# Attention and a rational feed-forward layer on one core: the numerator's constant is added on VectorE in the first part's units

## The chip, the cores and the metric

The kernel runs on one core of one Trainium2 chip. The core has a matrix engine (TensorE, "PE" in the profile; its weight loads are "PEld"), VectorE ("DVE"), ScalarE ("ACT"), GpSimd ("POOL") and SyncE ("SP", which only issues transfers). Each has its own list of instructions, which it works off in order; semaphores join the lists. SBUF is the on-chip memory, PSUM the memory into which TensorE writes, and the DRAM scratch tiles lie off the core.

The metric is device time in microseconds (us), lower is better. Before the change the median of 3 runs is 1245.48 us (1244.66 to 1249.6).

## The reference

Two layers, one behind the other. First block-causal attention over 8 batches of 8 heads, 576 positions, 64 numbers a head, with blocks of 64; then a feed-forward layer whose activation is a quotient of polynomials:

```
scores = q @ k.T / 8, masked where block(i) < block(j)
attn   = softmax(scores) @ v                 -> x, 4608 tokens x 512

h = x @ w_in                                 (512 -> 2048)
P = a[0] + a[1]*h + a[2]*h^2 + a[3]*h^3
Q = 1 + |b[0]|*|h| + |b[1]|*h^2
g = P / (Q + 1e-6)
out = g @ w_out                              (2048 -> 512)
```

## The kernel before

**Precision.** TensorE's fast format for fp32 keeps fewer bits than fp32. So nearly every operand x is held as a rounded part x_hi in that format and a remainder x_lo, and a product is three matmuls: hi by hi, hi by lo, lo by hi. For x, w_in and w_out these pairs are made once; for g they are made in each unit, as the tiles gh and gl.

**Attention.** 32 pairs of heads follow each other (p = 0 to 31). For each pair there are five row tiles and two halves, that is ten steps: scores on TensorE, the negative row maximum on VectorE (L542 to L548), the exponential on ScalarE (L560), the sums' reciprocal (L567 to L569) and the scaling on GpSimd (L572), a transposition on TensorE (L598), the split of the transposed tile on ScalarE (L611) and VectorE (L612), and the product with v on TensorE (L664), whose result is split again (L666, L667, L671) and stored to DRAM scratch xscr. The first EV = 5 pairs do without the split (L609, L621, L625). `bank` gives a PSUM tile to transpositions and to the preparation of the next pair: for p < LEND it goes in turn to the attention pool and to the two output banks o0 and o1, later to the attention pool alone.

**Feed-forward.** The 16 blocks of 128 hidden columns fall into two parts. The first part (ph = 0) is blocks 0 to 9, over chunks of 256 tokens, two blocks to a unit: 14 chunks of 5 units, 70 units, with a [128, 512] tile each. Its partial sums go to DRAM scratch pscr. The second part (ph = 1) has 74 units over chunks of 512 tokens, and runs behind attention. The units' steps are a generator, `Ffn.steps`, two half steps to a unit. A unit goes through `first` (24 matmuls of w_in, L229, and the start of P and Q), one unit later `recip`, two units later `split`, three units later `second` (the matmuls with w_out, L299).

The chain of one unit of the first part, in the names of the code, with h in PSUM and ut, vt, st tiles in SBUF:

```
first:  ACT  L236 ut = |h|         ACT L238 st = a3*h + a2     ACT L239 vt = b1*ut + b0
        POOL L243 ut = vt*ut       DVE L244 st = st*h          DVE L245 st = (st + a1)*h
recip:  ACT  L251 vt = Ln(ut + QC) ACT L258 vt = Exp(-vt)      (vt = 1/Q)
        ACT  L259 st = st + a0     DVE L260 gh = st*vt         (rounded)
        DVE  L261 ut = (ut + QC)*gh    POOL L263 ut = st - ut  (P - Q*gh)
split:  POOL L275 gl = ut*vt
second: PE   L299 o += gh.w_hi, gh.w_lo, gl.w_hi
```

In the second part the branch of `recip` is another one, and the change leaves it alone.

**What sets the order.** The loop over attention's steps emits half steps of `Ffn.steps` between them. Their number by a given step is a straight line, which ends at U1, where HOLD half steps are left out; what is held back is emitted after attention and works while the last pair's data is on its way:

```
E0, E1, U1 = there[0][0], there[-2][0], there[-2][1] * units_of(0, 0) * 2 - HOLD
```

The order of emission is not yet the order of execution. The kernel is built with `tile.TileContext(nc, schedule_with_timeline_sim=True)`: a planner with costs of its own for each instruction puts the lists of the engines in order and sets the semaphores. So an edit of one operation can move others, too. All transfers of attention and of the units are issued from SP's list (L214 loads a unit's x, L401 and L403 the next pair's q and k).

Of the kernel before, what the change touches and what calls it, by code (L numbers as in the profile page):

```python
# [8 lines left out]
F32 = mybir.dt.float32  # L9
# [3 lines left out]
AF = mybir.ActivationFunctionType  # L13
ALU = mybir.AluOpType
# [8 lines left out]
NCH = NT // CT  # L23
NF = DFF // 128
ALAG2 = 1
LEND = 4
RL = 3
C0 = 0
TP = 0
RW = 4  # L30
EV = 5
DP = 4
DN = (3, 0, 0, 0, 0)
KQB = 3
XB = 3
WR, WF = 1, 4
HOLD = 4
ALAG3 = 10
OFFS = (0,3,5)
TLAG = 6  # L40
# [27 lines left out]
QC = 1.0 + 1e-6  # L68
# [5 lines left out]
def attn_ffn_kernel(  # L74
# [11 lines left out]
    nc = tc.nc  # L86
# [27 lines left out]
    a0, a1 = coef[:, 0:1], coef[:, 1:2]  # L114
# [69 lines left out]
    class Ffn:  # L184
# [64 lines left out]
        def recip(self, ph, c, u):  # L249
            pool, ut, vt, st = self.m[ph, c, u]  # L250
            nc.scalar.activation(out=vt, in_=ut, func=AF.Ln, bias=qcb)  # L251
            tag = f"{ph}_{c}_{u}"
            gh, gl = (pool.tile([128, NBU[ph], CTS[ph]], F32R, name=f"g{x}{tag}", tag=f"g{x}",
                                bufs=GBUFS if pool is ffn else 2) for x in "hl")
            gf = gh.rearrange("p j t -> p (j t)")
            self.g[ph, c, u] = (gh, gl)
            if ph == 0:
                nc.scalar.activation(out=vt, in_=vt, func=AF.Exp, scale=-1.0)  # L258
                nc.scalar.activation(out=st, in_=st, func=AF.Identity, bias=a0)  # L259
                nc.vector.tensor_tensor(out=gf, in0=st, in1=vt, op=ALU.mult)  # L260
                nc.vector.scalar_tensor_tensor(out=ut, in0=ut, scalar=QC, in1=gf.bitcast(F32),  # L261
                                               op0=ALU.add, op1=ALU.mult)
                nc.gpsimd.tensor_tensor(out=ut, in0=st, in1=ut, op=ALU.subtract)  # L263
            else:
                r0 = ps_b.tile([128, 512], F32, name=f"r{tag}", tag="a", bufs=3)
                nc.scalar.activation(out=r0, in_=vt, func=AF.Exp, scale=-1.0)
                nc.vector.scalar_tensor_tensor(out=ut, in0=ut, scalar=QC, in1=r0, op0=ALU.add, op1=ALU.mult)
                nc.vector.scalar_tensor_tensor(out=r0, in0=ut, scalar=-2.0, in1=r0, op0=ALU.add, op1=ALU.mult)
                nc.vector.scalar_tensor_tensor(out=st, in0=st, scalar=a0, in1=r0, op0=ALU.subtract, op1=ALU.mult)
# [92 lines left out]
    with ExitStack() as actx:  # L362
# [27 lines left out]
        def load(p):  # L390
# [4 lines left out]
            tr = att.tile([128, 2, D], F32, name=f"tr{p}", tag="tr", bufs=1)  # L395
            if p >= EV:
                vr = att.tile([128, 2, 5, D], F32, name=f"vr{p}", tag="vr", bufs=1)
            for i, (raw, src) in enumerate(((qr, q), (kr, k))):
# [4 lines left out]
                eng.dma_start(out=tr[64 * i:64 * i + 64], in_=src[b, h0:h0 + 2, 512:S, :].rearrange("j p d -> p j d"))  # L403
            if p < EV:
                st_[p] = dict(qr=qr, kr=kr, tr=tr)
# [63 lines left out]
        def vprep(p):  # L469
            if p < EV:  # L470
                b, hp = divmod(p, NPAIR)
# [5 lines left out]
                return  # L477
            if p == EV:
                late()
# [13 lines left out]
        def bank(p, name):  # L493

            if p < LEND:
                nbank[0] += 1
# [92 lines left out]
        def transp(p, d):  # L589
            st_[p].pop(d)  # L590
            for gi, g in enumerate(groups(d)):
# [4 lines left out]
                for x, (i, h, kb) in enumerate(g):  # L596
                    src = pts[4] if i == 4 else pts[i][:, h]
                    nc.tensor.transpose(ps[:, 128 * x:128 * x + 128], src[:, 128 * kb:128 * kb + 128], ident)  # L598
                if p < EV:
                    if "pt" not in st_[p]:  # L600
# [6 lines left out]
                src = ps[:, :128 * n].rearrange(sh.get((g[0][0], n), "p (h k t) -> p h k t"), **kw)  # L607
                if p < EV:
                    nc.scalar.copy(out=spot(st_[p]["pt"], g), in_=src)  # L609
# [185 lines left out]
```

## Time and profile before

| | |
|---|---|
| median of 3 runs | 1245.48 us |
| the profiled execution's own time | 1246.05 us |
| its span, first to last instruction | 1244.3 us |
| PE busy / DVE / ACT / POOL | 1191.3 / 921.3 / 908.5 / 876.7 us |
| granted TensorE clock, mean | 0.994 |
| transferred | 145.67 MB, mean 117 GB/s |

The profile is of one execution. A group's row names its line, engine, operation, tiles (written <- read), shapes, count, then busy us and mean ns of one, then the idle time of the engine ahead of it and what ended that. A row of waits is "who <- for whom: us in total, times, longest". The chain of waits is followed back from the last instruction, at each step to what released it or to the instruction ahead of it on its engine. Matmuls are pipelined, so that their busy times overlap and a busy PE isn't PE at its peak.

### The profile page before, as it was taken

How to read it: one execution, taken by the hardware profiler on the slowest of the kernel's cores; microseconds unless marked ns; L12 is line 12 of the kernel's file. 1: busy time of each engine (PE TensorE's matmuls, PEld its weight loads, DVE VectorE, ACT ScalarE, POOL GpSimd, SP SyncE). 2: the span in 40 equal slices, each digit the busy share in tenths (PEclk: the TensorE clock that was granted, in tenths of full speed). 3: DMA queues.
4: the chain of work that ended last, by engine and by line, in shares of the span. 5: the costliest groups of instructions: out<-in, count | busy, mean ns of one | idle time of the engine just before them, and what ended most of it. 6: DMA issues, size and time to landing. Idle time of an engine off the chain costs nothing.

```text
span 1244.3 us, 21931 instructions
## 1 busy us (share of the span) xinstructions
PE 1191.3 (96%) x7124; PEld 1008.8 (81%) x7124; DVE 921.3 (74%) x2016; ACT 908.5 (73%) x2025; POOL 876.7 (70%) x1043
## 2 busy tenths in 40 slices
PE   6888999999999999999999999999999999999998
PEld 4666888888888878888888888878888888888886
DVE  6878888777888777877777777647666766677764
ACT  6877888877988878888888888756555655555554
POOL 4666778877888877787777877756665656665664
PEclk8999999999999999999999999999999999999999
DMA  8782344463544545443333342444014344443100
GB/s 233 208 232 71 94 138 113 121 179 89 143 114 132 132 125 143 108 136 100 100 103 92 105 110 68 113 154 189 1 64 131 120 136 136 136 136 102 43 1 34
DMA packets 199506, 145.67 MB, mean 117 GB/s; under 512 B 136288, under 2 KB 164960, under 8 KB 199392
## 3 DMA queue, kind: packets, MB, share of 16 engines
q1 hardware_dynamic: 196624, 143.15, 40.1%
q10 hardware_dynamic: 2704, 1.11, 0.3%
q8 instruction: 57, 0.93, 0.3%
q14 instruction: 57, 0.47, 0.1%
q0 software_dynamic: 64, 0.00, 0.0%
HBM read 92.28 MB, written 41.94 MB: 108 GB/s over the span
## 4 chain that ended last, share of the span: by engine, by line
PE 71%; ACT 8%; POOL 7%; DVE 5%; DMA 5%; issue 3%; SPq 1%; POOLq 0%; ACTq 0%; DVEq 0%
PE h L229 28%; PE o L299 26%; PE o L664 5%; PE t L598 4%; PE s L530 4%; ACT p L560 2%; PE o L625 2%; POOL gl L275 2%; DMA xt<-xh 1%; POOL u L263 1%; PE tp L438 1%; POOL p L572 1%; PE s L513 1%; DMA wri<-in_moe_w_in_dram 1%; DMA x<-xscr 1%
## 5 line engine op out<-in xcount | busy, mean ns | idle before, releaser
L229 PE MATMUL h<-x,wpi 128*128 128x256 f32 (+1 forms) x2568 | 453.6, 324 | 7.2 <-DMA x<-xscr 2.5
L229 PEld LDWEIGHTS h<-x,wpi 128*128 128x128 f32 x2568 | 380.7, 190 | 53.0 <-issue 6.0
L299 PE MATMUL o<-wpo,gh 128*128 128x512 f32 x1152 | 343.8, 395 | 0.0
L299 PEld LDWEIGHTS o<-wpo,gh 128*128 128x128 f32 x1152 | 212.8, 188 | 43.3 <-issue 0.7
L299 PE MATMUL o<-wpo,gl 128*128 128x512 f32 x576 | 210.3, 400 | 8.6 <-POOL gl L275 8.2
L572 POOL TENSOR_SCALAR p<-p,rc 128x128 f32<-128x128 f32 (+4 forms) x288 | 176.1, 623 | 48.4 <-DVE rc L569 32.9
L243 POOL TENSOR_TENSOR u<-v,u 128x512 f32<-128x512 f32 x144 | 187.5, 1302 | 13.2 <-ACT v L239 5.4
L560 ACT ACTIVATE p<-s,nm 128x288 f32<-128x288 f32 (+4 forms) x320 | 168.3, 534 | 25.2 <-DVE nm L548 19.9
L251 ACT ACTIVATE v<-u,qcb 128x512 f32<-128x512 f32 x144 | 105.1, 730 | 82.0 <-POOL u L243 81.7
L244 DVE TENSOR_TENSOR s<-s,h 128x512 f32<-128x512 f32 x144 | 98.5, 684 | 86.4 <-ACT s L241 65.2
L236 ACT ACTIVATE u<-h 128x512 f32<-128x512 f32 x144 | 86.4, 600 | 102.3 <-PE h L229 96.2
L548 DVE TENSOR_REDUCE nm<-s 128x1 f32<-128x128 f32 (+4 forms) x288 | 129.4, 474 | 7.4 <-PE s L513 4.7
L278 POOL TENSOR_TENSOR gl<-s,gh 128x512 fp32r<-128x512 f32 x74 | 95.8, 1294 | 55.0 <-ACT gh L277 54.9
L598 PE MATMUL t<-ident,p 128*128 128x128 f32 x800 | 122.5, 279 | 8.6 <-POOL p L572 4.1
L299 PEld LDWEIGHTS o<-wpo,gl 128*128 128x128 f32 x576 | 104.7, 189 | 31.1 <-POOL gl L275 12.4
L611 ACT CAST ptrh<-t 128x512 fp32r<-128x512 f32 (+1 forms) x189 | 98.4, 542 | 36.9 <-PE t L598 36.6
L612 DVE TENSOR_TENSOR ptrl<-t,ptrh 128x512 fp32r<-128x512 f32 (+1 forms) x189 | 115.5, 627 | 11.5 <-ACT ptrh L611 10.4
L242 POOL TENSOR_SCALAR v<-u,bab 128x512 f32<-128x512 f32 x74 | 57.2, 774 | 91.0 <-ACT u L236 90.9
L598 PEld LDWEIGHTS t<-ident,p 128*128 128x128 f32 x800 | 91.0, 141 | 27.8 <-POOL p L572 6.8
L263 POOL TENSOR_TENSOR u<-s,u 128x512 f32<-128x512 f32 x70 | 90.3, 1290 | 30.3 <-DVE u L261 16.2
L245 DVE SCALAR_TENSOR_TENSOR s<-s,coef,h 128x512 f32<-128x512 f32 x144 | 106.2, 738 | 2.4
L530 PE MATMUL s<-k,q 64*128 64x512 f32 (+3 forms) x768 | 86.4, 343 | 6.6 <-ACT p L560 2.9
(110 smaller groups left out, 2031.5 us busy)
## 6 DMA issues: line engine op xcount, KB each, us to landing
x<-xscr SPq DMA_DIRECT2D x44, 256.0 KB, 4.0
xscr<-xl SPq DMA_DIRECT2D x32, 288.0 KB, 2.4
out_dram<-os SPq DMA_DIRECT2D x34, 256.0 KB, 3.3
qr<-in_q_dram SPq DMA_DIRECT2D x64, 128.0 KB, 2.8
kr<-in_k_dram SPq DMA_DIRECT2D x62, 128.0 KB, 2.5
xt<-xh SPq DMA_DIRECT2D x54, 144.0 KB, 2.3
xscr<-xh SPq DMA_DIRECT2D x54, 144.0 KB, 2.5
pscr<-os SPq DMA_DIRECT2D x14, 512.0 KB, 2.7
```

The source lines that it names most:

```text
L229: nc.tensor.matmul(h[:, j, :], lhsT=w.win(f, dc, y), rhs=xs[dc][:, hl, :], start=(dc == 0 and i == 0), stop=(dc == 3 and i == 2))
L243: nc.gpsimd.tensor_tensor(out=ut, in0=vt, in1=ut, op=ALU.mult)
L245: nc.vector.scalar_tensor_tensor(out=st, in0=st, scalar=a1, in1=hf, op0=ALU.add if ph == 0 else ALU.subtract, op1=ALU.mult)
L251: nc.scalar.activation(out=vt, in_=ut, func=AF.Ln, bias=qcb)
L263: nc.gpsimd.tensor_tensor(out=ut, in0=st, in1=ut, op=ALU.subtract)
L299: nc.tensor.matmul(self.o[m], lhsT=g[:, j, ms], rhs=w.wout(f, y), start=(u == 0 and j == 0 and i == 0), stop=(u == nu - 1 and j == NBU[ph] ...
L530: mm = nc.tensor.matmul(s["s", t, h], lhsT=q[hs, x, 128 * t:128 * t + 128], rhs=k[hs, y, 0:128 * (t + 1)], start=(n == 0 and t == i), stop ...
L548: nc.vector.reduce_max(out=nm[:, j:j + 1], in_=s[d, j][:, :w] if i == 4 else s["s", i, j], axis=AX.X, negate=True)
L560: nc.scalar.activation(out=dst, in_=s.pop((d, j2))[:, :w] if i == 4 else s.pop(("s", i, j2)), func=AF.Exp, bias=nm[:, n:n + 1], scale=1.0, ...
L572: nc.gpsimd.tensor_scalar(out=x, in0=x, scalar1=rc[:, j2:j2 + 1], scalar2=1.0, op0=ALU.mult, op1=ALU.mult)
L598: nc.tensor.transpose(ps[:, 128 * x:128 * x + 128], src[:, 128 * kb:128 * kb + 128], ident)
L612: nc.vector.tensor_tensor(out=dl, in0=src, in1=dh.bitcast(F32), op=ALU.subtract)
```

## The change

In the first part's `recip`, st is no longer brought to P by an addition of its own. The two places that read P now read st and add a0 (a column of coef) themselves: the product that gives gh, and the subtraction that gives the remainder, which moves from GpSimd to VectorE. The ScalarE addition and the GpSimd subtraction are left out. `u % FUM < FUN` with both at 1 holds for every unit, so the old branch is never built. Two constants of the order are changed with it: LEND from 4 to 5 and HOLD from 4 to 3.

```diff
-LEND = 4
+LEND = 5
...
+FUM = 1
+FUN = 1
...
-HOLD = 4
+HOLD = 3
...
             if ph == 0:
                 nc.scalar.activation(out=vt, in_=vt, func=AF.Exp, scale=-1.0)
-                nc.scalar.activation(out=st, in_=st, func=AF.Identity, bias=a0)
-                nc.vector.tensor_tensor(out=gf, in0=st, in1=vt, op=ALU.mult)
-                nc.vector.scalar_tensor_tensor(out=ut, in0=ut, scalar=QC, in1=gf.bitcast(F32),
-                                               op0=ALU.add, op1=ALU.mult)
-                nc.gpsimd.tensor_tensor(out=ut, in0=st, in1=ut, op=ALU.subtract)
+                if u % FUM < FUN:
+                    nc.vector.scalar_tensor_tensor(out=gf, in0=st, scalar=a0, in1=vt, op0=ALU.add, op1=ALU.mult)
+                    nc.vector.scalar_tensor_tensor(out=ut, in0=ut, scalar=QC, in1=gf.bitcast(F32),
+                                                   op0=ALU.add, op1=ALU.mult)
+                    nc.vector.scalar_tensor_tensor(out=ut, in0=st, scalar=a0, in1=ut, op0=ALU.add, op1=ALU.subtract)
+                else:
+                    (the four lines above, as they were)
```

More of the change, by code (lines that the diff above doesn't have):

```diff
@@ L258, in recip @@
                 nc.scalar.activation(out=vt, in_=vt, func=AF.Exp, scale=-1.0)
-                nc.scalar.activation(out=st, in_=st, func=AF.Identity, bias=a0)
-                nc.vector.tensor_tensor(out=gf, in0=st, in1=vt, op=ALU.mult)
-                nc.vector.scalar_tensor_tensor(out=ut, in0=ut, scalar=QC, in1=gf.bitcast(F32),
-                                               op0=ALU.add, op1=ALU.mult)
-                nc.gpsimd.tensor_tensor(out=ut, in0=st, in1=ut, op=ALU.subtract)
+                if u % FUM < FUN:
[4 more added lines that the diff above has]
+                else:
+                    nc.scalar.activation(out=st, in_=st, func=AF.Identity, bias=a0)
+                    nc.vector.tensor_tensor(out=gf, in0=st, in1=vt, op=ALU.mult)
+                    nc.vector.scalar_tensor_tensor(out=ut, in0=ut, scalar=QC, in1=gf.bitcast(F32),
+                                                   op0=ALU.add, op1=ALU.mult)
+                    nc.gpsimd.tensor_tensor(out=ut, in0=st, in1=ut, op=ALU.subtract)
             else:
```

## The prediction

> **What bounds it now.** I read the page's totals and its chain first, then the busy time by stretch, then the groups of the lines that the change edits, then who waits for whom.
>
> ```profile
> span 1244.3 us, 21931 instructions
> PE 1191.3 (96%) x7124; PEld 1008.8 (81%) x7124; DVE 921.3 (74%) x2016; ACT 908.5 (73%) x2025; POOL 876.7 (70%) x1043
> PE 71%; ACT 8%; POOL 7%; DVE 5%; DMA 5%; issue 3%; SPq 1%; POOLq 0%; ACTq 0%; DVEq 0%
> ```
>
> The first two are the page's totals, the third the chain of waits by engine. The mean says "TensorE-bound", but it averages two stages. The 70 units that the change touches lie between 104 and 836 us, beside attention (rows below). The busy time by stretch (start and end, length, then busy us and instructions of PE, PEld, DVE, ACT and POOL, clock, DMA) separates the stages:
>
> ```profile
> 104.00:822.00 718.00, 694.01 (x4792) 605.24 (x4791) 566.06 (x1378) 592.66 (x1420) 561.24 (x700) 1.00 0.42 113
> ...
> 822.00:846.00 24.00, 21.42 (x104) 17.21 (x103) 10.22 (x15) 12.81 (x22) 13.44 (x12) 1.00 0.87 292
> 846.00:1244.00 398.00, 392.92 (x1734) 325.02 (x1732) 267.77 (x395) 223.46 (x365) 242.44 (x218) 1.00 0.27 90
> ```
>
> After 846 us TensorE works 392.92 of 398 us and every helper has room; nothing of the change runs there. From 104 to 822 us TensorE shows 694.0 of 718 us, and the three helpers stand close together: ScalarE 82.5%, VectorE 78.8%, GpSimd 78.2%. TensorE's busy time flatters it, since matmuls overlap. The chain of waits, asked for 104 to 846 us, gives its first lines their shares of 742 us:
>
> ```profile
> by line: PE h L229 20.1%; PE o L299 16.8%; PE o L664 8.5%; PE t L598 5.8%; PE s L530 5.6%; issue 3.2%; POOL gl L275 2.7%; DMA xt<-xh 2.4%; ACT p L560 2.3%; POOL u L263 2.2%; PE tp L438 2.0%; POOL p L572 1.6%; PE s L513 1.4%; POOL xl L671 1.
> ```
>
> The TensorE entries sum to about 60%, so some 40% of this stage is paced by other engines. L263, the GpSimd subtraction that the change takes away, is 2.2% of 742 us, 16.3 us, and L275, which runs behind it, another 20 us. So the stage is a balanced pipeline in which GpSimd's tail of each unit matters.
>
> **The operations.** These are the groups, with count, busy time, mean ns of one, and idle before:
>
> ```profile
> L244 DVE TENSOR_TENSOR s<-s,h 128x512 f32<-128x512 f32 x144 | 98.5, 684 | 86.4 <-ACT s L241 65.2 <-ACT s L238 20.7
> L245 DVE SCALAR_TENSOR_TENSOR s<-s,coef,h 128x512 f32<-128x512 f32 x144 | 106.2, 738 | 2.4
> L259 ACT ACTIVATE s<-s,coef 128x512 f32<-128x512 f32 x70 | 51.6, 738 | 9.9 <-DVE s L245 9.7
> L260 DVE TENSOR_TENSOR gh<-s,v 128x512 fp32r<-128x512 f32 x70 | 58.8, 840 | 17.1 <-ACT v L258 16.4
> L261 DVE SCALAR_TENSOR_TENSOR u<-u,gh 128x512 f32<-128x512 f32 x70 | 58.8, 840 | 2.3 <-DVE gh L260 0.9
> L263 POOL TENSOR_TENSOR u<-s,u 128x512 f32<-128x512 f32 x70 | 90.3, 1290 | 30.3 <-DVE u L261 16.2
> L275 POOL TENSOR_TENSOR gl<-u,v 128x512 fp32r<-128x512 f32 x70 | 91.0, 1300 | 2.3
> ```
>
> and the single-line views' smallest, median and largest duration:
>
> ```profile
> L244 DVE TENSOR_TENSOR s<-s,h x144: 662/686/691, 100.6 to 1229.4; 128x512 f32<-128x512 f32 x144
> L245 DVE SCALAR_TENSOR_TENSOR s<-s,coef,h x144: 661/746/750, 101.8 to 1230.1; 128x512 f32<-128x512 f32 x144
> L260 DVE TENSOR_TENSOR gh<-s,v x70: 666/693/2270, 106.6 to 833.4; 128x512 fp32r<-128x512 f32 x70
> L261 DVE SCALAR_TENSOR_TENSOR u<-u,gh x70: 665/693/2144, 107.4 to 834.2; 128x512 f32<-128x512 f32 x70
> ```
>
> Two things are to be seen. An operation whose added number comes from a column of coef (L245) has a median of 746 ns, one with a constant in the instruction (L261) 693. And L244, which reads one operand from PSUM, never strays beyond 691 ns, while L260 and L261, which read both from SBUF, average 840 - 693 = 147 ns over their median and reach 2270: now and then they are held up while running.
>
> *Removed on ScalarE:* 70 x 738 ns = 51.6 us (L259). It lies beside VectorE's and TensorE's work, and the exponential L258, not L259, is what L260 is seen waiting for. I take 0; the bounds are 0 and the 9.7 us in which ScalarE stood waiting for L245 ahead of L259.
>
> *Removed on GpSimd, added on VectorE:* 70 x 1290 ns = 90.3 us go. The new operation adds a column of coef and has both tensors in SBUF, a pairing that this trace does not hold; its bounds are L245's median of 746 ns and 746 + 147 = 893 ns, and I take 893 because its sources are L261's. That is 62.5 us. L260 becomes of that form too: 693 to 746, 53 ns x 70 = 3.7 us. VectorE gets 66.2 us; in the 104 to 822 us stretch, with 68 units, 64.3 us, to 630.4 of 718 us, 87.8%. ScalarE falls to about 75%, GpSimd to about 66%. What hides the addition is VectorE's 152 us idle there; without this cover the whole 64.3 us would count.
>
> *What it is worth on the path.* The removed step feeds L275, the remainder's product, and that feeds the second matmul. Who waits for it, in all:
>
> ```profile
> PEld o L299 <- POOL gl L275: 12.4, 15, 2.2
> PE o L299 <- POOL gl L275: 8.2, 11, 1.8
> ```
>
> TensorE stands 8.2 us in 11 waits for this product. The step before it becomes 1290 - 893 = 397 ns shorter, and it no longer queues on GpSimd, where L275 and attention's scaling stand in line: 8.2 / 11 = 0.75 us a wait is within 397 ns and one GpSimd slot. I take all 8.2 us. The bounds come from the chain: if the new operation replaces L263 wherever that stood, the 16.3 us shrink by 397 / 1290, 5.0 us; if nothing takes its place, by 16.3 us. A second reading gives a like size: each engine's time on the chain over its busy time (POOL 7% of 1244.3 = 87.1 of 876.7, 9.9%; ACT 99.5 of 908.5, 11.0%; DVE 62.2 of 921.3, 6.8%) times what it loses or gains is -8.9 - 5.7 + 4.5 = -10.1 us. I keep -8.2 since TensorE must turn an earlier release into time. For L260's dearer form I add 6.8% of 3.7 us, 0.3 us, between 0 and 3.7.
>
> *LEND 4 to 5:* attention pair 4 and the preparation of pair 5 may also use the two output banks, which the units first need at 109.6 us. The chain of waits shows the output matmuls of pairs 2 to 4, and what stands between the last two:
>
> ```profile
> 66.53 5.46 PE o L625 x20
> 84.47 5.62 PE o L625 x20
> 91.63 2.74 DMA xscr<-xl
> 94.42 2.78 DMA x<-xscr
> 103.67 5.62 PE o L625 x20
> ```
>
> Pair 4 comes 19.20 us behind pair 3, against 17.94 before, so about 1.3 us could be won. But the chain in between runs through a store and the reload of the first unit's input, 5.5 us, not through a bank. I take 0, bounds -1.3 and 0.
>
> *HOLD 4 to 3:* one half step of a unit moves from behind attention into it, its 24 matmuls or 12 of a second product with its three or four helper operations. Behind attention the chain waits for the last pair's transfers:
>
> ```profile
> 822.84 5.02 DMA xt<-xh
> 829.48 5.87 DMA xscr<-xl
> 835.40 2.07 DMA x<-xscr
> ```
>
> TensorE has 24 - 21.42 = 2.6 us idle there, filled otherwise by held steps. A half step is about 2.9 us by
>
> ```profile
> 568.91 2.86 PE h L229 x24
> 473.72 5.74 DMA x<-xscr
> ```
>
> so this is +2.9 us if the cover tears by that much, -2.6 if the step fills idle time earlier and the tail shrinks; I take 0.
>
> *Order:* the planner reorders every engine's list with its own costs. A transfer that another order exposes or hides is worth what the second row above shows, 5.7 us, of either sign; 0 in the sum. This change adds no DMA and moves only those that the half step issues.
>
> **Sum.** The profiled run took 1246.05 us, 1244.3 of them the span: 1246.05 - 8.2 + 0.3 = 1238.15. It lies 0.57 above the median, 1245.48, so the forecast is 1237.6 us.
>
> **The rivals.** *VectorE becomes the bound, and the kernel slower.* VectorE's waits in the 104 to 822 us stretch (us, times, longest), of which ScalarE and TensorE end:
>
> ```profile
> DVE xl L667 <- ACT xh L666: 26.3, 25, 2.2
> DVE s L244 <- ACT s L238: 19.2, 30, 1.7
> DVE s L542 <- PE s L530: 13.2, 22, 2.2
> DVE gh L260 <- ACT v L258: 10.9, 14, 1.8
> DVE ptrl L612 <- ACT ptrh L611: 10.4, 21, 0.9
> DVE xl L655 <- ACT xh L652: 7.4, 5, 2.2
> DVE s L525 <- ACT p L560: 6.3, 12, 1.1
> DVE nm L548 <- PE s L513: 3.3, 5, 1.2
> DVE nm L548 <- ACT p L560: 2.0, 5, 0.8
> ```
>
> They sum to 99.0 us. The added operation stands in VectorE's list ahead of attention's maxima and differences, for which ScalarE and TensorE wait in turn. If these waits stay whole, 630.4 + 99.0 = 729.4 us do not fit into 718: +11.4, or 1256.9 us by the median. It decides from 718 - 630.4 = 87.6 us of remaining waits on, 88% of the 99.0. For it: three such operations follow each other in a unit, in program order. Against it: ScalarE loses 7 points of its load, and most of these waits are for ScalarE.
>
> *The hold-ups multiply.* If three operations in a row with both operands in SBUF are each held up twice as long as today, 294 ns instead of 147, VectorE gets another 68 x 3 x 147 ns = 30.0 us, to 660.4; with the 99.0 us of waits that is 41.4 us over, 1286.9 us. Against it: GpSimd, which would hold them up, is busy 12 points less, and its 90.3 us of two-operand reading go. The Trainium skill, "SBUF — State Buffer", section "Who interferes with whom", says that a VectorE instruction with two SBUF inputs and a GpSimd instruction that reads SBUF block each other whole, whoever starts second waiting; that speaks against this change. The trace agrees in kind, by L244's 691 against L260's 2270 ns as largest duration.
>
> *It doesn't matter.* Another chain of the balanced stage, or a transfer such as the 5.74 us one, takes the place of L263: between -3 and +5 us, 1245.5 us. For it: TensorE shows only 24 us idle in 718.
>
> *All of it goes.* The subtraction's whole time leaves the chain: -16.3 + 0.3, 1229.5 us. For it: GpSimd's queue, where L275, attention's scaling and the transposed outputs wait behind each other, gets 12 points lighter.
>
> **How the numbers follow.** Forecast 45% (its own range 1233 to 1242), all of it goes 17%, it doesn't matter 22%, VectorE the bound 13%, hold-ups 3%. A measurement of this kernel can tell about 0.5%, 6.2 us, from no change. Of the forecast's 45%, 31 lie under 1239.3 and 14 above; of the 22%, one is faster, 18 same, 3 slower. Faster: 31 + 17 + 1 = 49%; same: 14 + 18 = 32%; slower: 3 + 13 + 3 = 19%. The range 1228 to 1254 leaves out the lower part of "all of it goes", the upper part of "VectorE the bound" and the hold-ups, under 20%.
>
> **What would show it.** GpSimd's busy time near 786 us, ScalarE's near 857, VectorE's near 987. The new operation near 893 ns and L260's successor near 893; medians near 746. TensorE's wait for gl under 3 us. No L263 on the chain, and VectorE's part of it at most 6%. I am wrong if VectorE's waits shrink little while its share passes 90%, if the three operations' means pass 1 us, if TensorE's idle in the stretch does not fall, or if the chain's share of DMA rises by what GpSimd's falls.

## The result and the profile after

The change makes the kernel slower: 1260.22 us, median of 6 runs (1255.65 to 1264.91), against 1247.24 us for the kernel before in the same session (1243.66 to 1249.6). The ratio is 1.0107, with an interval of 1.0074 to 1.0140. The forecast was 1237.6 us, its range 1228 to 1254. Time and direction were both wrong.

The profiled execution took 1263.93 us, 3.7 us above its median, with a span of 1262.2 against 1244.3 us. So the traces differ by 17.9 us, and the medians by 13.0: some of what follows belongs to this execution alone. In the kernel after, line numbers are 2 higher up to the changed branch and 8 higher behind it. The product gh is L262, the constant's product L263, the added subtraction L265, and GpSimd's gl L283.

The page's totals and the chain by engine:

```profile
span 1262.2 us, 21863 instructions
PE 1198.1 (95%) x7124; PEld 1014.4 (80%) x7124; DVE 982.5 (78%) x2086; ACT 873.8 (69%) x1955; POOL 799.5 (63%) x973
PE 68%; ACT 8%; DVE 8%; POOL 7%; DMA 4%; issue 3%; SPq 1%; POOLq 0%; ACTq 0%; DVEq 0%
```

Work moved as announced: ScalarE lost 34.7 us, GpSimd 77.2, and VectorE gained 61.2. But TensorE's part of the chain fell from 71 to 68%, and VectorE's rose from 5 to 8%.

Next the busy time by stretch, in the columns of the prediction. The last row of the kernel after is laid so that it holds the second part's 398 us, as the prediction's last row does for the kernel before. The kernel before:

```profile
0.00:104.00 104.00, 82.92 (x499) 61.31 (x500) 77.23 (x230) 79.54 (x221) 59.55 (x115) 0.97 0.76 209
104.00:820.00 716.00, 692.01 (x4780) 603.37 (x4778) 564.13 (x1376) 591.02 (x1418) 559.47 (x698) 1.00 0.42 113
```

and the kernel after:

```profile
0.00:104.00 104.00, 80.79 (x478) 60.28 (x478) 73.53 (x220) 75.49 (x210) 58.04 (x114) 0.93 0.74 207
104.00:820.00 716.00, 686.77 (x4725) 598.43 (x4724) 615.65 (x1432) 551.91 (x1339) 480.44 (x622) 0.99 0.42 113
864.00:1262.00 398.00, 392.78 (x1733) 325.00 (x1731) 267.74 (x392) 223.19 (x363) 240.58 (x216) 1.00 0.26 87
```

The second part is untouched: 392.78 us of TensorE's work in its 398, before 392.92. All is lost ahead of it. TensorE's count of matmuls tells about where. At 104 us it is 21 behind (478 against 499); from 104 to 820 us it falls another 55 back (4725 against 4780). At the pace of before, 4780 / 716 = 6.68 a us, that is 3.1 and 8.2 us. The rest of the 17.9 us, 6.6 by this estimate, is lost behind 820 us, in the handover to the second part. In the middle stretch TensorE's idle rose from 24.0 to 29.2 us, where it was to fall.

The wait that was to vanish, for GpSimd's product gl, in the waits of the kernel after:

```profile
PEld o L307 <- POOL gl L283: 20.0, 21, 2.3
POOL gl L283 <- DVE u L265: 17.5, 14, 3.3
PE o L307 <- POOL gl L283: 13.5, 17, 2.1
```

It grew, from 12.4 and 8.2 us before. GpSimd's own wait for VectorE is not what is new: before, its subtraction L263 stood waiting 16.2 us for L261, now gl waits 17.5 us for L265. By the trace's records, a unit takes 5.40 us in the mean from the start of gh to the end of gl, where it took 6.10, so this chain did get shorter. But the planner's order leaves less room behind it: from gl's end to the first matmul that reads it the median is 0.67 us, where it was 1.73.

The prices of the operations came out as estimated. These are the single-line views' smallest, median and largest duration in the kernel after:

```profile
L262 DVE SCALAR_TENSOR_TENSOR gh<-s,coef,v x70: 672/751/1746, 112.3 to 839.8; 128x512 fp32r<-128x512 f32 x70
L263 DVE SCALAR_TENSOR_TENSOR u<-u,gh x70: 664/693/2130, 113.2 to 841.3; 128x512 f32<-128x512 f32 x70
L265 DVE SCALAR_TENSOR_TENSOR u<-s,coef,u x70: 664/747/1850, 115.4 to 842.0; 128x512 f32<-128x512 f32 x70
```

and the same lines as groups, with busy time and mean:

```profile
L262 DVE SCALAR_TENSOR_TENSOR gh<-s,coef,v 128x512 fp32r<-128x512 f32 x70 | 56.1, 801 | 19.0 <-ACT v L260 18.6
L263 DVE SCALAR_TENSOR_TENSOR u<-u,gh 128x512 f32<-128x512 f32 x70 | 63.8, 911 | 1.5 <-DVE gh L262 0.2
L265 DVE SCALAR_TENSOR_TENSOR u<-s,coef,u 128x512 f32<-128x512 f32 x70 | 63.7, 910 | 0.5
```

The new operation takes 910 ns (893 forecast), and 0.5 us of idle stands ahead of all 70. The three hold VectorE for 801 + 911 + 910 ns = 2.6 us a unit, where before two operations of 840 ns held it for 1.7 us. What stands behind all three in VectorE's list comes up to 0.9 us later. They are not one block here: in 64 of the 70 units the planner has put one to five other operations of VectorE between the second and the third, and only in one unit do all three follow each other directly. The chain by line, from 104 to 864 us, shares of 760 us:

```profile
by line: PE h L231 17.5%; PE o L307 15.7%; PE o L672 9.7%; PE t L606 5.2%; PE s L538 4.6%; POOL gl L283 3.8%; issue 3.8%; ACT p L568 2.9%; POOL p L580 2.4%; DVE u L263 2.1%; DVE gh L262 1.7%; DVE u L265 1.6%; POOL u L245 1.6%; POOL xl L679 
```

GpSimd's subtraction (2.2% of 742 us, 16.3 us) is gone from the chain. The three VectorE operations hold 2.1 + 1.7 + 1.6 = 5.4%, 41 us, where the two of before, L260 and L261, held 6.5 + 5.8 = 12.3 us, and gl grew from 2.7% of 742 (20 us) to 3.8% of 760 (29 us).

Last, the handover. Attention's last product with v, in the single-line view of the kernel before:

```profile
L664 PE MATMUL o<-ptrl,vst x270: 272/309/499, 130.6 to 821.4; 128*128 128x512 f32 x27, 128*128 128x320 f32 x27, 128*128 128x64 f32 x27, 128*128 128x448 f32 x27
```

and after:

```profile
L672 PE MATMUL o<-ptrl,vst x270: 272/309/499, 135.1 to 839.4; 128*128 128x512 f32 x27, 128*128 128x320 f32 x27, 128*128 128x64 f32 x27, 128*128 128x448 f32 x27
```

It starts at 839.4 instead of 821.4 us, 18.0 us later, as much as the whole loss in these two traces. The units had not slipped as far: their last added operation starts at 842.0 us, 7.0 us behind the last GpSimd subtraction of before:

```profile
L263 POOL TENSOR_TENSOR u<-s,u x70: 1258/1290/1305, 109.7 to 835.0; 128x512 f32<-128x512 f32 x70
```

So less of the units' work is left to stand behind attention. The chain of the kernel after there:

```profile
844.45 6.11 DMA xscr<-xl
857.21 7.89 PE h L231 x24
```

and its busy time by stretch:

```profile
848.00:852.00 4.00, 1.50 (x7) 0.92 (x5) 0.00 (x0) 1.17 (x2) 0.00 (x0) 0.94 0.36 132
852.00:856.00 4.00, 2.90 (x6) 1.82 (x6) 0.32 (x1) 1.60 (x3) 0.76 (x1) 0.50 0.97 287
```

The store of the last pair lies open, TensorE works 1.50 of 4 us beside it, and then runs at half its clock.

### The profile page after: what moved, and what is told of

Same layout as the page of the kernel before. It is cut to its first block, busy times and chain, and to the rows that moved or that the text cites. A ratio compares the mean times of both kernels' runs of the same rounds, so it can differ in the third digit from the quotient of the medians.

```text
span 1262.2 us, 21863 instructions
## 1 busy us (share of the span) xinstructions
PE 1198.1 (95%) x7124; PEld 1014.4 (80%) x7124; DVE 982.5 (78%) x2086; ACT 873.8 (69%) x1955; POOL 799.5 (63%) x973
## 4 chain that ended last, share of the span: by engine, by line
PE 68%; ACT 8%; DVE 8%; POOL 7%; DMA 4%; issue 3%; SPq 1%; POOLq 0%; ACTq 0%; DVEq 0%
PE h L231 26%; PE o L307 25%; PE o L672 6%; PE t L606 3%; PE s L538 3%; ACT p L568 2%; POOL gl L283 2%; PE o L633 2%; POOL p L580 1%; DVE u L263 1%; PE tp L446 1%; DVE gh L262 1%; DVE nm L556 1%; DVE u L265 1%; POOL u L245 1%
## 5 line engine op out<-in xcount | busy, mean ns | idle before, releaser
L231 PE MATMUL h<-x,wpi 128*128 128x256 f32 (+1 forms) x2568 | 460.2, 326 | 12.1 <-DMA x<-xscr 8.3
L231 PEld LDWEIGHTS h<-x,wpi 128*128 128x128 f32 x2568 | 385.0, 192 | 57.4 <-issue 8.5
L307 PE MATMUL o<-wpo,gh 128*128 128x512 f32 x1152 | 349.4, 396 | 0.2 <-DVE gh L262 0.2
L307 PE MATMUL o<-wpo,gl 128*128 128x512 f32 x576 | 214.8, 402 | 13.5 <-POOL gl L283 13.5
L580 POOL TENSOR_SCALAR p<-p,rc 128x128 f32<-128x128 f32 (+4 forms) x288 | 186.0, 657 | 58.7 <-DVE rc L577 47.8
L283 POOL TENSOR_TENSOR gl<-u,v 128x512 fp32r<-128x512 f32 x70 | 90.2, 1289 | 33.3 <-DVE u L265 17.5
L275 DVE SCALAR_TENSOR_TENSOR u<-u,r 128x512 f32<-128x512 f32 x74 | 50.7, 686 | 67.0 <-ACT r L274 65.6
```

The source lines that it names most:

```text
L231: nc.tensor.matmul(h[:, j, :], lhsT=w.win(f, dc, y), rhs=xs[dc][:, hl, :], start=(dc == 0 and i == 0), stop=(dc == 3 and i == 2))
L283: nc.gpsimd.tensor_tensor(out=gl, in0=ut, in1=vt, op=ALU.mult)
L307: nc.tensor.matmul(self.o[m], lhsT=g[:, j, ms], rhs=w.wout(f, y), start=(u == 0 and j == 0 and i == 0), stop=(u == nu - 1 and j == NBU[ph] ...
L580: nc.gpsimd.tensor_scalar(out=x, in0=x, scalar1=rc[:, j2:j2 + 1], scalar2=1.0, op0=ALU.mult, op1=ALU.mult)
```

## The experiments

Two questions were to be told apart. Is the added VectorE work itself the cost, and by what way: its throughput, the hold-ups by GpSimd, or the delay of what is queued behind it? Or is it the planner's new order, or one of the two constants? A line with each diff says what is changed against which kernel; "fused" is the new branch with LEND and HOLD as before, 4 and 4. All ratios are to the kernel before on the same chip.

### One part at a time

Fused alone; the constants alone; the fused branch without its third operation; and with the subtraction back on GpSimd, without a0 in it. The third kernel leaves out the remainder's subtraction, the fourth a0's part of it.

```diff
 # e1_fusion_only: the new branch, constants as before
+FUM = 1
+FUN = 1
 # e2_constants_only: the old branch
-LEND = 4
+LEND = 5
-HOLD = 4
+HOLD = 3
 # e3_no_third: as e1, without
-                    nc.vector.scalar_tensor_tensor(out=ut, in0=st, scalar=a0, in1=ut, op0=ALU.add, op1=ALU.subtract)
 # e4_subtract_on_gpsimd: as e1, but
-                    nc.vector.scalar_tensor_tensor(out=ut, in0=st, scalar=a0, in1=ut, op0=ALU.add, op1=ALU.subtract)
+                    nc.gpsimd.tensor_tensor(out=ut, in0=st, in1=ut, op=ALU.subtract)
```

> The change's fused operations with LEND and HOLD as they were before (4 and 4). Theory 'VectorE full' (the 66 us added to VectorE set the pace of the attention stage): 1256 to 1262 us, VectorE busy near 982 us. Theory 'constants' (LEND 5 moves the first reload, HOLD 3 thins the cover behind attention): 1240 to 1249 us. Theory 'order' (the planner's new lists are worse by chance, whatever the load): anywhere from 1240 to 1265, no rule.

> Before with LEND 5 and HOLD 3, nothing fused. 'VectorE full': 1244 to 1250 us, like before. 'Constants': 1254 to 1262 us. 'Order': away from before by up to 6 us on either side, although no engine's load differs.

> e1 with the third VectorE operation left out (the remainder is then not taken from P, so the second product's low part holds another number): ScalarE -51.6 us, GpSimd -90.3 us, VectorE only +3.7 us. 'VectorE full': below before, 1232 to 1244 us. 'Order': 1245 to 1262 us. If even this is no faster than before, ScalarE's and GpSimd's relief is worth nothing on the path.

> e1 with the subtraction back on GpSimd, without a0 in it (that part of the remainder is left out): ScalarE -51.6 us, GpSimd as before, VectorE +3.7 us. 'VectorE full': 1240 to 1247 us, a little under before by ScalarE's relief. 'Order': 1240 to 1260 us.

| kernel | median us | ratio | interval |
|---|---|---|---|
| fused alone | 1264.11 | 1.0157 | 1.0125 to 1.0189 |
| constants alone | 1267.68 | 1.0174 | 1.0139 to 1.0209 |
| fused, third operation left out | 1242.07 | 0.9968 | 0.9946 to 0.9990 |
| fused, subtraction on GpSimd | 1253.8 | 1.0073 | 1.0048 to 1.0097 |

Each of the two halves of the change costs at least as much as the whole, so they don't add up; this is taken up below. The constants alone lie above every range that was expected for them. The third kernel is the one that speaks: with ScalarE's addition and GpSimd's subtraction both gone, and nothing put in their place on VectorE, only 0.3% is won. That is what was there of the gain the forecast was after, in the one order that was tried; as this kernel, too, has an order of its own, it isn't a strict ceiling. Its busy time by stretch:

```profile
104.00:820.00 716.00, 700.74 (x4841) 611.71 (x4840) 581.09 (x1383) 558.22 (x1358) 477.60 (x634) 1.00 0.43 116
```

The stage's pace is better than before (4841 matmuls against 4780), and its chain is 77% TensorE's. From there the third operation costs 1264.11 - 1242.07 = 22 us, a third of the 63 us for which it runs. The fourth kernel warns against putting all of this down to VectorE: nothing was added there but the dearer form of the first operation, some 4 us, GpSimd has its subtraction as before, and still it loses 0.7%. Its order is a new one, too.

### The constants

```diff
 # e5_lend5, e6_hold3, e12_before_hold8: the old branch with one constant changed
+LEND = 5        (e5)
+HOLD = 3        (e6)
+HOLD = 8        (e12)
 # e7_fused_lend5, e8_fused_hold3, e9_fused_hold8: the same in the fused branch
```

> Before with LEND 5 alone. e2 (LEND 5, HOLD 3, nothing fused) was 23 us slower than before with the same work on every engine. Theory 'LEND': 1260 to 1270 us, and e6 like before. Theory 'HOLD': like before, 1241 to 1250 us. Theory 'fitted order' (before's list is a lucky one among many, and any nudge leaves it): this one and e6 both 1250 to 1270 us, neither adding up to e2.

> Before with HOLD 3 alone. 'LEND': 1241 to 1250 us. 'HOLD': 1260 to 1270 us. 'Fitted order': 1250 to 1270 us.

> The fused operations with LEND 5 and HOLD 4. The fused kernel with (4, 4) took 1264 us, with (5, 3) 1260 us. 'VectorE full': 1256 to 1266 us whatever the constants, since the load is the same. 'Fitted order': scatters as the unfused ones do, between 1245 and 1275 us.

> The fused operations with LEND 4 and HOLD 3, the last of the eight combinations. 'VectorE full': 1256 to 1266 us. 'Fitted order': between 1245 and 1275 us, and the mean of the four fused ones within 6 us of the mean of the four unfused ones.

> The fused operations with LEND 4 and eight half steps held back behind attention instead of four. In the four fused kernels TensorE stands some 8 us longer than before in the handover behind attention, where the last pair's stores and reloads are waited for: attention ends 15 to 20 us later, the units 6 to 10, so little unit work is left to cover. Theory 'handover': the four half steps (2.9 us each) cover it, 1252 to 1258 us, against 1264 with four held. 'VectorE full' alone (the pace of the stage): 1259 to 1266 us.

> Before with HOLD 8, the control of e9. Before's handover leaves TensorE only 3.4 us idle: 'handover' gives 1243 to 1252 us here, no gain. If this one falls as far as e9 does, holding back helps by something else than the cover. 'Fitted order': 1250 to 1265.

Medians in us, with the ratio behind them:

| LEND / HOLD | old branch | fused |
|---|---|---|
| 4 / 4 | 1244.5 to 1248.4 (five groups of runs) | 1264.11, 1.0157 |
| 4 / 3 | 1250.61, 1.0026 | 1261.86, 1.0108 |
| 5 / 4 | 1262.11, 1.0093 | 1260.25, 1.0097 |
| 5 / 3 | 1267.68, 1.0174 | 1260.22, 1.0107 (the change) |
| 4 / 8 | 1259.62, 1.0092 | 1256.85, 1.0074 |

In the old branch every other setting tried costs time, LEND 5 alone nearly as much as the change. In the fused branch all five lie within 7.3 us. The stage's pace with LEND 5 alone shows how (the old branch):

```profile
0.00:104.00 104.00, 82.26 (x492) 61.61 (x493) 73.99 (x223) 75.47 (x211) 58.05 (x114) 0.95 0.76 207
104.00:820.00 716.00, 684.06 (x4688) 595.35 (x4687) 557.83 (x1362) 585.57 (x1405) 550.87 (x689) 0.99 0.42 113
```

Pair 4's banks matter up to about 110 us. At 104 us only 7 matmuls are missing; from there to 820 us, behind the place where LEND acts directly, 92 are. A change of a constant in the first tenth of the kernel reorders the rest of it: by line and tile, TensorE's first 353 matmuls are the same in the two traces, and of all 7124 only 3580 stand in the same place of its list. The kernel before is the fastest of the ten in this table. That its constants were fitted to its own order, so that any edit starts with a loss, is the likeliest reading, but it is not shown. How much of the change's 13 us is the order, the pinned orders below ask.

HOLD 8 helps the fused branch, by 7 us against HOLD 4, as the handover's lack of held work would have it. TensorE's busy time from 820 to 866 us is 42.42 of 46, against 39.17 with HOLD 4 (43.42 before). HOLD 8's row:

```profile
820.00:866.00 46.00, 42.42 (x210) 35.00 (x210) 29.72 (x47) 27.43 (x49) 23.00 (x23) 0.96 0.63 226
```

In the old branch, whose cover is not thin, HOLD 8 wins nothing and costs 0.9%. The change's step from 4 to 3 went the wrong way for the handover, but at its own size (1264.11 to 1261.86, 1260.25 to 1260.22) it can't be told from nothing.

### Is it VectorE's load

If VectorE's busy time were the bound, taking work off it would help. One piece that ScalarE can take is the fill of masked scores, 22 us.

```diff
 # e13_fused_fill_on_act and e14_fill_on_act_hold8: fused (HOLD 4 and 8); e16_before_fill_on_act: the old branch
-                        nc.vector.memset(m, NEG)
+                        nc.scalar.activation(out=m, in_=m, func=AF.Copy, scale=0.0, bias=NEG)
 # e15_half_fused: every second unit takes the new branch
+FUM = 2
+FUN = 1
```

> The fused kernel (4, 4), with the fill of masked scores (192 fills, 22 us on VectorE) moved to ScalarE, which the fusion relieved by 52 us. 'VectorE's load': the relief counts some 0.46 us a us, as between e3, e11, e1 and e10: 10 us, 1250 to 1257 us. 'Fitted order': a new draw, 1252 to 1268 us, no rule by the load.

> e13 with eight half steps held back. If 'VectorE's load' and 'handover' are both right and add: 1242 to 1250 us, near or under before. 'Fitted order': 1250 to 1265 us.

> Every other unit fused, constants (4, 4): VectorE +33 us instead of +66, ScalarE -26, GpSimd -45. 'VectorE's load': between before and e1, 1250 to 1258 us. 'Fitted order': 1255 to 1268 us, no better than the fully fused ones.

> Before with the fill of masked scores on ScalarE: VectorE -22 us, ScalarE up by its 192 short operations. 'VectorE's load' (VectorE as the one bound): 1235 to 1245 us. 'Fitted order' (any edit leaves the fit): 1250 to 1268 us, like the other four unfused ones with edits.

The three with the fill on ScalarE took 1281.61 us (1.0263, 1.0235 to 1.0292), 1275.64 (1.0213, 1.0184 to 1.0241) and 1269.29 (1.0155, 1.0109 to 1.0201), by the ratios 13 to 19 us more than their partners without, and above both ranges that were expected of each. Freed VectorE time was no gain where another engine took a place in attention's chain for it; the fill's group in the first of them shows ScalarE standing still ahead of it, for the scores:

```profile
L550 ACT ACTIVATE s<-s 64x64 f32<-64x64 f32 (+1 forms) x192 | 32.7, 204 | 31.8 <-PE s L538 31.4
```

These kernels, each with a new order, don't hold ScalarE's added wait apart from VectorE's relief, so they refute only the plain form, that VectorE's sum of work sets the time. Half fused took 1258.41 us (1.0072, 1.0045 to 1.0098), about half of the loss of the fully fused kernel (1.0157). That is what a price for each operation would give; but the table of constants scatters by as much, so it is no proof.

### What the third operation costs, and by what

Two kernels keep the fused branch's first two operations and give VectorE a third whose result nobody reads: once the same operation, with its result into a dead tile, once a maximum over one tile, of like length and with one SBUF input. Then gl needs only the second operation, as in the kernel without a third.

```diff
 # e10_dead_third: as e1, but
-                    nc.vector.scalar_tensor_tensor(out=ut, in0=st, scalar=a0, in1=ut, op0=ALU.add, op1=ALU.subtract)
+                    nc.vector.scalar_tensor_tensor(out=st, in0=st, scalar=a0, in1=ut, op0=ALU.add, op1=ALU.subtract)
 # e11_dead_lockfree: as e1, but
+                    nc.vector.reduce_max(out=st[:, 0:1], in_=st, axis=AX.X)
```

> The fused kernel (4, 4) with the third VectorE operation kept, same inputs and place, but writing to st, which nobody reads any more (so the remainder's product takes the second operation's result): VectorE's load stays, the unit's chain gets one step shorter. Theory 'VectorE's load': 1257 to 1266 us, like e1. Theory 'the unit's chain': 1240 to 1250 us, like e3.

> As e10, but in its place a maximum over st into one column, a VectorE operation of like length with one tensor input instead of two, that nobody waits for. 'VectorE's load': 1254 to 1264 us, at most the hold-ups' 10 us below e10. 'Hold-ups' (operations with two SBUF inputs against GpSimd): 1240 to 1250 us.

The maximum: 1258.91 us, 1.0089 (1.0059 to 1.0119). The dead subtraction: 1298.56 us, 1.0402 (1.0370 to 1.0434), far above both ranges that were expected. The two operations' single-line views, first that of the kernel with the maximum:

```profile
L265 DVE TENSOR_REDUCE s<-s x70: 665/676/683, 109.9 to 810.9; 128x1 f32<-128x512 f32 x70
```

then that of the kernel with the dead subtraction:

```profile
L265 DVE SCALAR_TENSOR_TENSOR s<-s,coef,u x70: 662/1318/3904, 108.4 to 856.1; 128x512 f32<-128x512 f32 x70
```

The same input size, but with two SBUF inputs: the median doubles, and the longest is six times the shortest. The place differs as well. The maximum stands directly behind the second operation in 66 of the 70 units, the dead subtraction in 2; elsewhere one to five other operations stand between, so that in 51 units it starts while gl, which the second operation released on GpSimd, is running. These take 1.58 us in the mean, and the ten that start while GpSimd runs nothing 0.82. The maximum takes 0.68 us beside a running GpSimd operation and 0.67 without. Nobody reads the dead subtraction's result, and still its kernel loses 40 us against the maximum's. The Trainium skill, "SBUF — State Buffer", section "Who interferes with whom", has it that a VectorE operation with two SBUF inputs and a GpSimd operation that reads SBUF exclude each other, and that one with a single input doesn't meet it: the maximum's 665 to 683 ns and the subtraction's 662 to 3904 agree. In the change itself GpSimd waits for the third operation, so this unit's gl can't run beside it, and its mean stays at 910 ns. Its hold-ups are near those of before: 163 ns over its median, where L260 and L261 had 147.

By ratios, the loss comes in these steps: no third operation 0.9968; a third that only occupies VectorE 1.0089; the true third, held up now and then and waited for by GpSimd, 1.0157. Occupying VectorE for 47 us (70 x 676 ns) is the largest step, +1.2%. Each of these kernels has its own order, so the steps are no surer than the scatter of the table of constants. Where the maximum's kernel loses its time can be seen: from 104 to 820 us it does as many matmuls as the kernel before, and it drops behind in the handover:

```profile
104.00:820.00 716.00, 692.92 (x4792) 605.49 (x4792) 606.39 (x1442) 555.89 (x1350) 473.55 (x630) 1.00 0.43 115
820.00:866.00 46.00, 31.91 (x140) 25.13 (x139) 20.30 (x35) 17.95 (x35) 16.39 (x17) 0.87 0.61 211
```

TensorE works 31.91 of 46 us there. The units end early (their last maximum starts at 810.9 us), but attention is late; its last products stand in the chain at

```profile
832.06 3.51 PE o L672 x11
```

so that little is left to work beside the last pair's transfers.

### The operations and the order, apart

Each of the kernels so far has an order of its own from the planner, and the table of constants shows that this alone moves the time. Two kernels pin the order of every engine's list: the new operations in the lists of the kernel before, and the old operations in the lists of the fused kernel. An operation that changes its engine, or has no partner, stands right behind the one that was emitted before it.

```diff
 # e17_fused_in_old_lists: the kernel is built twice; the second build's lists follow the first's
+LIST, OPS = False, True
+    _, told, made, added = build(LIST, None)
+    nc, _, _, _ = build(OPS, (told, made, set(added)))
 # e18_old_ops_in_fused_lists
+LIST, OPS = True, False
```

> The fused operations (constants 4 and 4) with every engine's list pinned to the one that the planner makes for before; the moved subtraction stands on VectorE right behind the product in front of it, the added constant's operation is gone. Theory 'the list' (what is lost is lost by the other order): 1235 to 1250 us, at or under before. Theory 'the operations' (VectorE's 66 us and their hold-ups cost by themselves): 1256 to 1268 us, like e1.

> The reverse: before's operations with every engine's list pinned to e1's, ScalarE's addition behind the unit's exponential, GpSimd's subtraction behind the product in front of it. 'The list': 1256 to 1275 us. 'The operations': 1243 to 1252 us, like before.

| operations | lists of before | lists of the fused kernel |
|---|---|---|
| old | 1246.91 | 1311.44, 1.0517 (1.0490 to 1.0543) |
| new | 1260.3, 1.0104 (1.0082 to 1.0125) | 1264.11, 1.0157 |

So "it is only the order" falls: in the order of before the new operations still cost 1.0%, as the change does. They run as well in it as in their own (1260.3, 1264.11), while the old operations lose 64 us in the other's, more than either theory expected. That the old order was made for the old operations may be a part of the 1.0%; these two kernels don't tell this part apart. In the first pinned kernel the lists are nearly the same but for the edit: in the traces TensorE's 7124 matmuls and ScalarE's 1955 remaining operations stand in the order of before, and of VectorE's 2016 old ones 33 stand one or two places off. The third operation stands directly behind the second in all 70 units, in the change in 6. So the waits can be compared one by one. First, with the new operations in the old lists, the groups of the second matmul and of attention's exponential:

```profile
L307 PE MATMUL o<-wpo,gl 128*128 128x512 f32 x576 | 211.3, 402 | 2.9 <-POOL gl L283 2.9
L568 ACT ACTIVATE p<-s,nm 128x288 f32<-128x288 f32 (+4 forms) x320 | 167.5, 529 | 65.8 <-DVE nm L556 53.7 <-DVE nm L552 10.5 <-PE tp L450 0.4
```

then its chain by engine, from the page, and by line from 104 to 857 us:

```profile
PE 57%; DVE 22%; ACT 10%; issue 4%; DMA 4%; POOL 3%; SPq 0%; ACTq 0%; DVEq 0%; POOLq 0%
...
by line: PE h L231 11.9%; PE o L307 10.1%; PE o L672 6.0%; issue 5.1%; DVE nm L556 5.1%; DVE ptrl L620 4.9%; ACT p L568 4.1%; DVE u L263 4.1%; DVE u L265 3.8%; DVE gh L262 3.4%; PE t L606 3.3%; PE s L538 3.1%; DVE s L247 2.6%; DVE s L246 2.
```

The same two groups in the kernel before:

```profile
L299 PE MATMUL o<-wpo,gl 128*128 128x512 f32 x576 | 210.3, 400 | 8.6 <-POOL gl L275 8.2
L560 ACT ACTIVATE p<-s,nm 128x288 f32<-128x288 f32 (+4 forms) x320 | 168.3, 534 | 25.2 <-DVE nm L548 19.9 <-DVE nm L544 4.4
```

and from its waits from 104 to 836 us, GpSimd's scaling for VectorE's reciprocal:

```profile
POOL p L572 <- DVE rc L569: 28.5, 63, 1.4
```

The forecast's first half is there for the most part: TensorE's wait for gl falls from 8.2 to 2.9 us. What it left out is there as well: the exponential's wait for VectorE's maximum grows from 19.9 to 53.7 us, and GpSimd's scaling now waits 63.9 us in the same stretch, 28.5 before; from the waits with the lists pinned:

```profile
POOL p L580 <- DVE rc L577: 63.9, 79, 3.1
```

VectorE's part of the chain rises from 5 to 22%. The three operations hold 3.4 + 4.1 + 3.8 = 11.3% of 753 us, 85 us, and the maximum and the split of attention, which stand behind them, another 10.0%. The loss is all within the stage: 4705 matmuls between 104 and 820 us against 4780, 75 / 6.68 = 11.2 us, the difference of the two spans (1255.5 and 1244.3):

```profile
104.00:820.00 716.00, 687.69 (x4705) 597.36 (x4704) 613.92 (x1426) 544.80 (x1332) 476.13 (x625) 0.99 0.42 113
```

In the other pinned kernel the old operations meet lists that don't expect GpSimd's long way, and TensorE's wait for gl is 49.0 us:

```profile
PE o L307 <- POOL gl L283: 49.0, 38, 2.9
```

A wait of an idle engine is not by itself a loss: in the kernel without the third operation the exponential also waits 37.4 us for the maximum, and that kernel is the fastest:

```profile
L567 ACT ACTIVATE p<-s,nm 128x288 f32<-128x288 f32 (+4 forms) x320 | 168.3, 534 | 46.0 <-DVE nm L555 37.4 <-DVE nm L551 7.7
```

It is the chain that says which waits count, and there VectorE has 6% in that kernel and 22% in the pinned one.

## Why the prediction was wrong

**The step that failed** is the claim "What hides the addition is VectorE's 152 us idle there", and with it the price of 0 for 66.2 us of added VectorE work on the path, of which only L260's 0.3 us were counted. Idle time of 152 us in 718 was there, but not where that work falls. VectorE serves two chains in one list. The units' piece of it grew from 1.7 to 2.6 us, and attention's maxima, reciprocals and splits behind it came later by up to 0.9 us. With the order held, the loss is 13.4 us in the medians (1260.3 against 1246.91), the gain on gl already in it. The prediction had asked what waits for the removed step; it had not asked, row by row, who waits for VectorE's other work, though it listed VectorE's own waits under a rival.

**gl earlier, -8.2 us.** The mechanism was right and is shown with the order held (8.2 to 2.9 us). In the change it came out the other way, 8.2 to 13.5: the chain from gh to gl is 0.7 us shorter there, but in the planner's new order the matmul that reads gl follows closer behind it (0.67 against 1.73 us). The bound of -16.3 was far off: with both removed operations left out and no third in their place, the gain is 0.3%, some 4 us.

**Second reading, -10.1 us.** It priced VectorE at 6.8%, its mean share of chain over busy time. L260 and L261 had more already before: 12.3 us of chain for 117.6 us of work, 10%. In the change the three operations have 41 us of chain for 183.6 us of work (56.1 + 63.8 + 63.7), 22%; in the pinned kernel 85 us. The share was no property of the engine: it rises with the work added.

**Prices.** The new operation 910 ns (893 forecast), medians 747 and 751 (746), VectorE's sum 982.5 us (987). L260's successor has a mean of 801 (893). ScalarE stands at 873.8, forecast 857, GpSimd at 799.5, forecast 786. GpSimd's 13 us are mostly its scaling of attention's rows, which takes 657 ns in the mean where it took 623, 10 us in all. The groups, before:

```profile
L572 POOL TENSOR_SCALAR p<-p,rc 128x128 f32<-128x128 f32 (+4 forms) x288 | 176.1, 623 | 48.4 <-DVE rc L569 32.9 <-DVE s L542 4.4 <-DVE k L421 2.9
```

and after:

```profile
L580 POOL TENSOR_SCALAR p<-p,rc 128x128 f32<-128x128 f32 (+4 forms) x288 | 186.0, 657 | 58.7 <-DVE rc L577 47.8 <-DVE k L429 2.9 <-DVE s L533 2.8
```

The same number of the same operations got longer, so it looks as if the hold-ups go both ways. ScalarE's 17 us are mostly a matter of counting. Of L259's 51.6 us, 13.1 lay over the records of the ScalarE operations next to it, and busy time counts such time once, so that only 38.5 us could go with it.

**LEND, 0 (-1.3 to 0).** Wrong in sign where it can be seen alone: +0.9% in the old branch, through the order of all that follows. In the fused branch it goes the other way (1.0157 to 1.0097, with intervals that don't meet), so the constant has no price of its own. The 21 matmuls that the change lacks at 104 us are not LEND's alone: with LEND 5 by itself 7 are missing, in the fused branch 1. The bounds came from the one place in which the constant acts directly. Why the planner's order gets that much worse from it stays open.

**HOLD, 0 (-2.6 to +2.9).** +0.3% in the old branch (3.2 us, 1.4 to 5.1 by the interval), nothing that can be told in the fused one. The range held within the noise. But its cover was judged by the handover of before; the change thins that cover out by itself, as attention ends later than the units do, and HOLD 8 won 7 us there.

**Order, 0, of either sign.** Of one sign in these runs: of nine other settings of the two branches none lies below the kernel before. The prediction let one transfer of 5.7 us stand for the order; in the old branch the time moves by 0.9% for LEND alone and by 1.7% for both constants, without any work added.

**The rivals.** "VectorE becomes the bound", 13%, had 1256.9 us and the right place: the added operation stands ahead of attention's maxima. That it lies near the measured time is in part luck, since its sum was not what happened. It wanted the waits of VectorE that ScalarE and TensorE end to stay whole and the load plus these to pass the stretch. VectorE worked 615.65 of 716 us, 86.0%, under the 90% named, and those waits did shrink, all nine of the forecast's list together from 99.0 to 68.2 us. Its four largest stand, in the waits of the kernel after from 104 to 820 us, at

```profile
DVE gh L262 <- ACT v L260: 18.4, 23, 1.8
DVE xl L675 <- ACT xh L674: 14.8, 20, 2.3
DVE s L246 <- ACT s L240: 14.1, 26, 1.5
DVE s L550 <- PE s L538: 11.5, 11, 6.0
```

or 58.8 us, against 10.9 + 26.3 + 19.2 + 13.2 = 69.6 before. VectorE is late, not full. Nor do the three operations follow each other as this rival had it: in the change only one unit in 70 has them side by side. "The hold-ups multiply" did not come true in the change (147 ns over the median before; 50, 218 and 163 after, the second from 911 - 693), since a unit's gl waits for its third operation instead of running beside it. The dead subtraction shows how near it was: there gl did run beside it, and the kernel lost 40 us against the maximum's. "It doesn't matter" and "all of it goes" fall with the result.

**What would show it.** Of the signs named for being wrong one came true, TensorE's idle in the stretch (24.0 to 29.2 us); the others (90%, means over 1 us, DMA's part of the chain) did not. VectorE's part of the chain, at most 6% by the forecast, was 8%.

**What stays open.** How the 13 us of the change as such divide between the operations and the order: with the old order held the operations cost all of it, the planner's orders for them are no better, and the two constants cost nothing on top of the fusion; but the kernel with the subtraction back on GpSimd loses 0.7% with hardly any work added to VectorE. And how far single hold-ups, rather than the plain length of the three operations, delay attention: the kernels with a one-input and the true third operation differ by 0.7%, but also in who waits for it. No version that computes the same was found to beat the kernel before.

## What to carry to other kernels

Before work is moved to an engine with idle time, list who waits for that engine's other work, and ask whether the moved piece stands ahead of them in the same list: added work there can delay them even where the engine has a fifth of its time free. Estimate the gain first by leaving the work out altogether, here 0.3%, and compare it with the scatter that an edit brings through the planner, here 0.3 to 1.7% for constants alone. To tell an edit from the order that comes with it, build the new operations into the old lists.

## What the runs showed of the hardware that was not expected

A VectorE operation with two SBUF inputs, which in 51 of 70 cases started while GpSimd's gl was running, takes 1318 ns in the median and up to 3904, where one with a single input takes 665 to 683. The longest is 3.2 us over that, more than two of GpSimd's operations of 1290 ns: waiting for a single one doesn't explain it. Three GpSimd operations lay beside it, for 3.4 us of its time.

A short hole can cost TensorE more than the hole. In the handover of the change's trace TensorE stood 3.23 us for a transfer, by the timeline:

```profile
852.73 2.90 PE L231 MATMUL h<-x,wpi 128*128 128x512 f32 x6 [3.23 <-DMA x<-xscr]
```

and the granted clock was 0.50 from 852 to 860 us. The busy time of the first half of that stretch stands above; the second half's:

```profile
856.00:860.00 4.00, 2.79 (x7) 2.22 (x8) 3.65 (x6) 2.82 (x5) 3.31 (x3) 0.50 1.02 417
```

The unit's 24 matmuls behind it take 7.89 us in the chain; at this place in the chain of the kernel before they take 5.78:

```profile
841.46 5.78 PE h L229 x24
```

The Trainium skill, "TensorE: Matmul & The Clock Gate", Part 1, gives about 3.4 us of idleness as what halves the clock. The traces here show it with less. In the change the granted clock fell at 851.5 us, 2.0 us after the end of the last matmul ahead of the hole. In the kernel before, a hole of 1.79 us, in which TensorE waited for gl, was followed by half the clock 1.1 us after its end; by the timeline and the busy time by stretch:

```profile
289.93 0.49 PE L299 MATMUL o<-wpo,gl 128*128 128x512 f32 x1 [1.79 <-POOL gl L275]
291.00:294.40 3.40, 3.40 (x15) 2.60 (x12) 2.81 (x9) 2.51 (x6) 1.86 (x4) 0.50 0.01 2
```

The clock is 0.50 over these 3.4 us, in which TensorE is busy throughout. So a wait of TensorE can cost more than its length in the table of waits, even where it is well below 3.4 us.
